# Pooled attention feeding a top-1 mixture of experts: one load moved forward, routing operations moved behind subtractions, one low-part subtraction moved to an earlier step, three more tiles stored undivided

## The chip, the cores and the metric

The kernel runs on one core of one Trainium2 chip. The metric is the device time of one execution in microseconds (us). Lower is better. The engines are named as in the profile: PE is TensorE (matrix products and transposes), DVE is VectorE, ACT is ScalarE, POOL is GpSimd, SP is SyncE, which here only issues DMAs. A DMA is a transfer between the chip's memory and an engine's memory.

## What is computed

The input q, k and v have 8 batches, 8 heads, 576 rows and 64 columns. Keys and values are averaged over groups of 8 rows, which leaves 72 of each. The attention's output is one row of 512 numbers for each of 4608 tokens. Each token then goes to the one expert of eight with the largest logit, through that expert's two matrices, and the result is scaled by the gate.

```python
k_p = k.reshape(B, H, Sp, 8, D).mean(axis=3)          # 72 pooled keys
v_p = v.reshape(B, H, Sp, 8, D).mean(axis=3)
scores = scale * np.matmul(q, k_p.transpose(0, 1, 3, 2))
scores = scores - np.max(scores, axis=-1, keepdims=True)
attn = np.exp(scores)
attn = attn / (np.sum(attn, axis=-1, keepdims=True) + 1e-09)
x = np.matmul(attn, v_p)                                # 4608 x 512 after a transpose
logits = x @ w_gate + modality_bias[modality_id]
e_idx = np.argmax(logits, axis=1)
probs = np.exp(logits - logits.max(-1, keepdims=True))
probs /= probs.sum(-1, keepdims=True) + 1e-09
gate_w = probs[np.arange(N), e_idx]
for e in range(8):
    mask = e_idx == e
    out[mask] = gate_w[mask, None] * (np.maximum(x[mask] @ w1[e], 0.0) @ w2[e])
```

## The kernel before, in words

The kernel has two stages that follow one another on PE. Roughly the first 180 us are attention and routing, the rest are the experts.

**Attention** runs in 20 steps, two batches to five steps. In each group of five, steps 0 and 1 are the two halves of the even batch, step 2 is a mixed step with the last 64 rows of both batches, and steps 3 and 4 are the halves of the odd batch. A step has two tiles of 128 tokens, a mixed step has one. Each step handles its scores in two halves of heads, w = 0 and w = 1. What a step does, with the names that the profile prints:

- `q_pe`, `q_act` transpose queries (`pq`, L578) and copy them (`qt`, L584).
- `s_pe` forms the scores (`sc`, L603; L597 in a mixed step).
- `s_dve` takes their maximum (`mx`, L610) and subtracts it (`sb`, L613) on DVE.
- `s_act` takes exponentials (`pe`, L625 and L626) on ACT.
- `t_pe`, `t_act` transpose them (`pp`, L632) and copy them (`pt`, L637). `t4_pe` transposes the remainder (L644) into free columns of the score tile of w = 0, so it waits until L613 has read that tile.
- `a_pe` multiplies with the values (`av`, L667 and L671). There is one `av` tile, so the next `a_pe` waits until `x_dve` has read the last one.
- `x_dve` reads `av`: the row sums (`r`, L690), their reciprocal (L694), the logits (`lg`, L696), and two multiplications that divide the rows (`xb`, L700). A tile called late skips L700: ACT copies the undivided rows (L692), the reciprocal is stored beside them in column RX and following, and the rows are multiplied by it after they have been gathered for an expert. L696 of a late tile comes after ACT's copy.

Keys and values of a batch are pooled mostly on POOL (`fold`, L351 to L353), partly on DVE (L356), and turned into operands on PE (`pk` L396 and L401, `pv` L443 and L444).

**The order of the work** is written out by hand. One loop over the steps calls these functions, and tables called hooks (`hook_0` to `hook_3`, `hook_q`) say what else is emitted at which point of which step. Every engine runs its instructions in the order in which they are emitted. The DMAs of all inputs are issued by SP, in one queue, from the table `step_loads`.

**Routing** of a group of nine tiles (one group for two batches) is some 30 small DVE operations. They stand in a list, `drip`. A call of `gap(n)` takes the next n of them and emits them at that place, unless the next one is held for PE. Group 0's list starts at step 6, group 1's at step 11, with a table for the first two slots of tokens behind it, group 2's at step 16. Group 3's is run in the expert stage.

**Experts.** Weights are used as two parts, a high part rounded on ACT (`split0`, L902) and a low part that DVE subtracts (`split_lo`, L141, 128x1024). The table over `hook_3` says in which step each of the eight pieces of the first expert has its low part made. From about 180 us on PE multiplies tokens in slots of 256, in the same pattern to the end (L183, L209, L214, L1345).

Of the kernel before, what the change touches and what calls it, by code (L numbers as in the profile page):

```python
# [14 lines left out]
AF = mybir.ActivationFunctionType  # L15
# [7 lines left out]
P = 128  # L23
SLOT = 256
EARLY_GROUPS = 2
# [8 lines left out]
def kernel(  # L34
# [12 lines left out]
    nc = tc.nc  # L47
# [3 lines left out]
    E, _, FF = w1.shape  # L51
# [187 lines left out]
    with ExitStack() as actx:  # L239
# [306 lines left out]
        def gap(n=2):  # L546

            for _ in range(n):
                if drip and drip[0] not in held:
                    drip.pop(0)()  # L550
# [55 lines left out]
        def s_dve(n, w):  # L606
            nh = 2 * len(steps[n][2])
            scv = scs.pop((n, w))[:, :, 0:nh * SPL].rearrange("p u (h s) -> p u h s", s=SPL)
            mx = ap.tile([P, 2, 4], F32, tag="mx", bufs=2, name=f"mx_{n}_{w}")[:, :, 0:nh]
            nc.vector.reduce_max(mx, scv, axis=AX.X)  # L610
            gap()
            sb = ap.tile([P, 2, 4 * SPL], F32, tag="sb", bufs=2, name=f"sb_{n}_{w}")
            nc.vector.tensor_tensor(sb[:, :, 0:nh * SPL].rearrange("p u (h s) -> p u h s", s=SPL), scv,  # L613
                                    mx.rearrange("p u (h o) -> p u h o", o=1).to_broadcast([P, 2, nh, SPL]), op=ALU.subtract)
            scs[n, w] = sb

        def s_act(n, w):
# [55 lines left out]
        def x_dve(t):  # L673
# [12 lines left out]

            late = g >= EARLY_GROUPS and z == 1
            r = xw[:, z, RX:RX + H].rearrange("p (u h) -> p u h", u=2) if late else s8
            rb = r.rearrange("p u (h o) -> p u h o", o=1)
            nc.vector.tensor_scalar(s8, avv[:, :, :, VC - 1], float(POOL), 1e-9 * POOL, op0=ALU.mult, op1=ALU.add)  # L690
            if late:
                nc.scalar.copy(xo.rearrange("p (u h d) -> p u h d", u=2, h=4), avv[:, :, :, 0:HD])  # L692
            gap(1)
            nc.vector.reciprocal(r, s8)  # L694
            gap(1)
            nc.vector.tensor_tensor(lgs[g][:, gi].rearrange("p (u h) e -> p u h e", u=2), avv[:, :, :, HD:HD + E],  # L696
# [34 lines left out]
        def route(g):  # L731
# [3 lines left out]
            lg = small("lgr", g, [P, n, E])  # L735
            ex = small("ex", g, [P, n, E])
            m1 = small("m1", g, [P, n])
# [8 lines left out]
            V = nc.vector  # L746
# [8 lines left out]
            def sub():  # L755
                V.tensor_tensor(lg, lg, per_e(m1, n), op=ALU.subtract)
                nc.scalar.activation(ex, lg, AF.Exp)
            add(sub)
# [20 lines left out]
            add(lambda: V.reduce_sum(sm, ex, axis=AX.X))  # L779
            add(lambda: V.tensor_scalar_add(sm, sm, 1e-9))  # L780
            add(lambda: V.reduce_sum(dc, oh[:, sl, :].rearrange("p t e -> p e t"), axis=AX.X))
# [134 lines left out]
        for f, n in enumerate((12, 13, 14, 15, 15, 16, 17, 19)):  # L916
            at(hook_1, n, lambda f=f: split0(f, 0))
            at(hook_2, n, lambda f=f: split0(f, 1))
        for f, n in enumerate((15, 15, 16, 16, 17, 17, 18, 19)):
            at(hook_3, n, lambda f=f: split_lo(f, nc.vector))  # L920
# [17 lines left out]
        step_loads = {}  # L938
        for n, fn, b in ((0, load_k, 2), (0, load_k4, 2), (0, load_v, 2), (0, load_v4, 2), (0, load_k, 3), (1, load_q, 2),
                         (1, load_v, 3), (1, load_k4, 3), (1, load_routing, None), (1, load_k, 4), (2, load_qmix, 1),  # L940
# [256 lines left out]
    for i, r in enumerate(EXTRA):  # L1197
# [14 lines left out]
    late = {  # L1212
        (0, 0): [lr[9], lr[7], lr[11], lr[8]],
        (0, 1): [lr[10]],
        (0, 3): [counts, lr[12]] + [fn for pair in zip(bases, lr[13:20]) for fn in pair] + lr[20:25],
        (0, 4): experts,
        (0, 5): lr[25:] + columns,
        (0, 6): first_cols[:3],
# [432 lines left out]
```

## Time and profile before

| | |
|---|---|
| three runs | 591.69, 593.76 and 594.55 us, median 593.76 |
| the profiled execution's own time | 590.98 us |
| its span, first to last instruction | 589.3 us |
| busy: PE, DVE, ACT, POOL | 97%, 63%, 46%, 32% |
| mean granted PE clock | 0.998 of full speed |

The profile lists instructions by engine, line and tile. A row of a timeline gives the start, the duration, the engine, the line, the operation, the tile written and the tiles read, the size and the count of merged instructions. In square brackets stands how long the engine sat idle before it, and whose work ended that. The view of waits sums these idle times. SP's rows are the issue of a DMA, not the transfer. In the order of the program, as against the trace, rows carry no time.

### The profile page before, as it was taken

How to read it: one execution, taken by the hardware profiler on the slowest of the kernel's cores; microseconds unless marked ns; L12 is line 12 of the kernel's file. 1: busy time of each engine (PE TensorE's matmuls, PEld its weight loads, DVE VectorE, ACT ScalarE, POOL GpSimd, SP SyncE). 2: the span in 40 equal slices, each digit the busy share in tenths (PEclk: the TensorE clock that was granted, in tenths of full speed). 3: DMA queues.
4: the chain of work that ended last, by engine and by line, in shares of the span. 5: the costliest groups of instructions: out<-in, count | busy, mean ns of one | idle time of the engine just before them, and what ended most of it. 6: DMA issues, size and time to landing. Idle time of an engine off the chain costs nothing.

```text
span 589.3 us, 12333 instructions
## 1 busy us (share of the span) xinstructions
PE 570.9 (97%) x3539; PEld 499.6 (85%) x3539; DVE 372.7 (63%) x945; ACT 273.8 (46%) x652; POOL 187.2 (32%) x290
## 2 busy tenths in 40 slices
PE   6999999999999999999999999999999999999995
PEld 5789789988898888888888888888888888888894
DVE  5877898788966766557455446855455487555311
ACT  2767677788552333333333336633333474334210
POOL 7679967765000323112112102112102113212101
PEclk9999999999999999999999999999999999999999
DMA  8999979995311744232232277242234843241101
GB/s 257 306 323 282 360 219 309 304 313 171 103 54 39 263 169 121 79 125 91 82 118 95 86 230 241 91 125 91 87 111 137 255 158 105 91 146 54 38 3 55
DMA packets 83426, 92.60 MB, mean 157 GB/s; under 512 B 17871, under 2 KB 58319, under 8 KB 83344
## 3 DMA queue, kind: packets, MB, share of 16 engines
q1 hardware_dynamic: 77424, 72.24, 39.2%
q0 software_dynamic: 5920, 19.44, 9.9%
q8 instruction: 30, 0.49, 0.4%
q14 instruction: 52, 0.43, 0.2%
HBM read 123.06 MB, written 27.58 MB: 256 GB/s over the span
## 4 chain that ended last, share of the span: by engine, by line
PE 82%; DVE 7%; DMA 5%; ACT 2%; issue 1%; SPq 1%; POOLq 0%; POOL 0%; DVEq 0%; ACTq 0%
PE op L1345 33%; PE hp L209 20%; PE hp L214 10%; PE av L667 4%; PE hp L183 3%; PE sc L603 3%; DMA q<-in_q_dram 3%; PE av L671 2%; DMA v<-in_v_dram 2%; PE pp L632 2%; PE pq L578 2%; PE ph L183 1%; DVE mx L610 1%; DVE hl L141 1%; DMA out_dram<-obw,slw 1%
## 5 line engine op out<-in xcount | busy, mean ns | idle before, releaser
L209 PE MATMUL hp<-xhl,hl 128*128 128x512 f32 x512 | 126.6, 390 | 0.0
L1321 POOL DMA_INDIRECT out_dram<-ob,sidx x34 | 36.8, 1083 | 263.6 <-DVE ob L1315 191.2
L209 PEld LDWEIGHTS hp<-xhl,hl 128*128 128x128 f32 x512 | 96.1, 188 | 19.9
L217 ACT COPY ht<-hp 128x256 f32<-128x256 f32 x128 | 47.3, 373 | 138.7 <-PE hp L214 112.3
L218 DVE TENSOR_TENSOR ht<-ht,hp 128x256 f32<-128x256 f32 x128 | 52.8, 420 | 92.5 <-ACT ht L217 89.4
L1345 PE MATMUL op<-hl,hx 128*128 128x512 f32 x429 | 104.8, 392 | 0.0
L1345 PEld LDWEIGHTS op<-hl,hx 128*128 128x128 f32 x429 | 78.5, 189 | 14.6
L1345 PE MATMUL op<-hl,hh 128*128 128x512 f32 x256 | 79.8, 393 | 0.0
L214 PEld LDWEIGHTS hp<-xhl,hl 128*128 128x128 f32 x512 | 69.8, 191 | 4.9
L214 PE MATMUL hp<-xhl,hl 128*128 128x256 f32 x512 | 71.5, 283 | 0.0
L1345 PEld LDWEIGHTS op<-hl,hh 128*128 128x128 f32 x256 | 46.0, 189 | 7.8
L667 PE MATMUL av<-vw,pt 128*128 128x146 f32 (+1 forms) x320 | 49.2, 293 | 1.4 <-DVE xb L700 1.3
L1345 PE MATMUL op<-hl,hlo 128*128 128x512 f32 x128 | 49.9, 390 | 0.0
L144 POOL DMA_INDIRECT xg<-xs,gidx x36 | 38.6, 1073 | 29.0 <-DMA raw<-in_moe_w_dram 13.8
L667 PEld LDWEIGHTS av<-vw,pt 128*128 128x128 f32 (+1 forms) x320 | 39.6, 180 | 3.4 <-DVE xb L700 1.0
L223 DVE SCALAR_TENSOR_TENSOR hx<-ht,hx 128x256 fp32r<-128x256 f32 x64 | 27.2, 427 | 18.8 <-DVEq L1350 15.7
L223 DVE SCALAR_TENSOR_TENSOR hlo<-ht,hh 128x256 fp32r<-128x256 f32 x64 | 27.1, 425 | 18.5 <-DVEq L1350 15.3
L603 PE MATMUL sc<-kt,qt 128*128 128x144 f32 x256 | 37.4, 289 | 0.6 <-DVE rs L798 0.3
L603 PEld LDWEIGHTS sc<-kt,qt 128*128 128x128 f32 x256 | 33.2, 190 | 1.6 <-DVE rs L798 0.5
L610 DVE TENSOR_REDUCE mx<-sc 128x8 f32<-128x576 f32 (+1 forms) x40 | 27.7, 692 | 7.5 <-PE sc L603 6.9
L671 PE MATMUL av<-vw,pt 128*128 128x146 f32 (+1 forms) x160 | 30.0, 290 | 0.0
L221 ACT ACTIVATE hx<-ht 128x256 fp32r<-128x256 f32 x64 | 26.2, 419 | 7.4 <-DVE ht L218 5.7
(279 smaller groups left out, 907.7 us busy)
## 6 DMA issues: line engine op xcount, KB each, us to landing
raw<-in_moe_w_dram SPq DMA_DIRECT2D x288, 256.0 KB
xs<-xb SPq DMA_DIRECT2D x16, 528.0 KB
scr<-xg SPq DMA_DIRECT2D x29, 256.0 KB
k<-in_k_dram SPq DMA_DIRECT2D x7, 1024.0 KB
v<-in_v_dram SPq DMA_DIRECT2D x7, 1024.0 KB
q<-in_q_dram SPq DMA_DIRECT2D x7, 1024.0 KB
y<-scr SPq DMA_DIRECT2D x108, 64.0 KB
v<-in_v_dram SPq DMA_DIRECT2D x16, 128.0 KB
```

Source lines behind the costliest of these rows:

```text
L144: nc.gpsimd.indirect_dma_start(out=x, out_offset=None, in_=xs[0:rows, :], in_offset=IndirectOffsetOnAxis(idx[:, col:col + 1].bitcast(U32), 0),
L209: nc.tensor.matmul(hp[g % 2], hl[g][:, 0, d * P:(d + 1) * P], ab[:, d, :, 0:SLOT], start=(d == 0), stop=False)
L214: nc.tensor.matmul(hp[g % 2][:, 0:SLOT], hl[g][:, 1, d * P:(d + 1) * P], ab[:, d, 0, 0:SLOT], start=False, stop=(d == ND - 1))
L217: nc.scalar.copy(hts[g % 2], hp[g % 2][:, SLOT:2 * SLOT])
L218: nc.vector.tensor_add(hts[g % 2], hts[g % 2], hp[g % 2][:, 0:SLOT])
L223: nc.vector.scalar_tensor_tensor(hlo, hts[g % 2], 0.0, hh.bitcast(F32), op0=ALU.max, op1=ALU.subtract)
L603: nc.tensor.matmul(dst, qt[:, i, :], kt[b % NB][:, :, h * SPL:(h + 1) * SPL], start=True, stop=True)
L610: nc.vector.reduce_max(mx, scv, axis=AX.X)
L667: nc.tensor.matmul(av[hs, u, 2 * VC * gg:2 * VC * (gg + 1)], pt[:, c, hs], vw[y][:, c].rearrange("p a x -> p (a x)"), start=(gg == 0), sto ...
L671: nc.tensor.matmul(dst4[hs], pt4[:, hs], v4[y][:, 2 * u:2 * u + 2, :], start=False, stop=True)
L1321: nc.gpsimd.indirect_dma_start(out=out[:, :], out_offset=IndirectOffsetOnAxis(idx.bitcast(U32), 0), in_=ob, in_offset=None, bounds_check=N ...
L1345: nc.tensor.matmul(ot, l[:, ts_], hl[f][:, w, D:2 * D], start=(f == 0 and n == 0), stop=(f == NF - 1 and n == 2))
```

## The change

Six edits, all in the attention stage and its routing:

1. **Loads.** The queries of batch 2 (`load_q`, 2) are issued ahead of the keys of batch 3 (`load_k`, 3). Before, the keys stood in step 0's row and the queries in step 1's.
2. **`s_dve`.** For w = 0 the two routing operations of `gap()` come behind the subtraction L613; before they stood between the maximum and the subtraction. For w = 1 nothing changes.
3. **`x_dve`.** Two routing operations come ahead of the row sums, in place of one behind the row sums and one behind the reciprocal. The two at the function's end stay.
4. **Late tiles.** The first tile of the last three steps (17, 18 and 19) is late too: its two multiplications L700 go, a copy on ACT comes.
5. **Routing.** The small constant added to the sum of exponentials (L780) goes. The tile `ex` gets a ninth column with that constant, which POOL writes when the group's list is made, and the sum (L779) runs over nine columns.
6. **Low parts.** The first of the eight low-part subtractions moves from step 15 to step 13. The others shift with it: steps 13, 15, 15, 16, 16, 17, 18, 19 in place of 15, 15, 16, 16, 17, 17, 18, 19, so step 17 has one in place of two.

```diff
@@ s_dve
             nc.vector.reduce_max(mx, scv, axis=AX.X)
-            gap()
+            if w:
+                gap()
...
             scs[n, w] = sb
+            if w == 0:
+                gap()
@@ x_dve
-            late = g >= EARLY_GROUPS and z == 1
+            late = g >= EARLY_GROUPS and (z == 1 or n >= N - 3)
...
+            gap(2)
             nc.vector.tensor_scalar(s8, avv[:, :, :, VC - 1], float(POOL), 1e-9 * POOL, op0=ALU.mult, op1=ALU.add)
...
-            gap(1)
             nc.vector.reciprocal(r, s8)
-            gap(1)
@@ route
-            ex = small("ex", g, [P, n, E])
+            ex = small("ex", g, [P, n, E + 1])
+            nc.gpsimd.memset(ex[:, :, E:E + 1], 1e-9)
...
-                nc.scalar.activation(ex, lg, AF.Exp)
+                nc.scalar.activation(ex[:, :, 0:E], lg, AF.Exp)
...
-            add(lambda: V.tensor_scalar_add(sm, sm, 1e-9))
@@ the tables
-        for f, n in enumerate((15, 15, 16, 16, 17, 17, 18, 19)):
+        for f, n in enumerate((13, 15, 15, 16, 16, 17, 18, 19)):
             at(hook_3, n, lambda f=f: split_lo(f, nc.vector))
...
-        for n, fn, b in (... (0, load_v4, 2), (0, load_k, 3), (1, load_q, 2),
+        for n, fn, b in (... (0, load_v4, 2), (1, load_q, 2), (1, load_k, 3),
```

The list of group 3, which runs in the expert stage, is one operation shorter as well, and its indices there shift by one.

What this does to the order of three queues follows. The lines of the changed kernel stand two or three numbers lower in the file: L614 there is L613 here, L694 is L690, L697 is L694, L702 is L700, L782 is L779, L783 is L781, L786 is L784, L794 is L792, L811 is L809.

DVE at the turn from step 6 to step 7, in group 0's routing, before: `mx` and `sb` are the maximum and subtraction of step 7, w = 0; `sm`, `dc`, `gate` and `cum` are routing; `r`, `lg` and `xb` belong to the second tile of step 5.

```order
L610 TENSOR_REDUCE mx_0_1100<-sc_0_1088 128x2x2
L779 TENSOR_REDUCE sm_1008<-ex_1005 128x9
L780 TENSOR_SCALAR sm_1008<-sm_1008 128x9
L613 TENSOR_TENSOR sb_0_1104<-sc_0_1088,mx_0_1100 128x2x144
L690 TENSOR_SCALAR r_1121<-av_1114 128x8
L781 TENSOR_REDUCE dc_1009<-oh 128x8
L694 RECIPROCAL r_1121<-r_1121 128x8
L784 RECIPROCAL gate<-sm_1008 128x9
L696 TENSOR_TENSOR lg_1071<-av_1114,r_1121 128x64
L700 TENSOR_TENSOR xb_171<-av_1114,r_1121 128x256 x2
L792 TENSOR_TENSOR cum<-cum,dc_1009 128x8
```

The same place in the changed kernel:

```order
L610 TENSOR_REDUCE mx_0_1101<-sc_0_1089 128x2x2
L614 TENSOR_TENSOR sb_0_1103<-sc_0_1089,mx_0_1101 128x2x144
L782 TENSOR_REDUCE sm_1009<-ex_1005 128x9
L783 TENSOR_REDUCE dc_1010<-oh 128x8
L786 RECIPROCAL gate<-sm_1009 128x9
L794 TENSOR_TENSOR cum<-cum,dc_1010 128x8
L694 TENSOR_SCALAR r_1122<-av_1115 128x8
L697 RECIPROCAL r_1122<-r_1122 128x8
L698 TENSOR_TENSOR lg_1072<-av_1115,r_1122 128x64
L702 TENSOR_TENSOR xb_171<-av_1115,r_1122 128x256 x2
```

The subtraction has moved two places forward. Four routing operations, `cum` among them, now stand between it and the row sums `r`, where one stood.

DVE at the turn from step 13 to step 14, before: `mx_0` and `sb_0` are step 14, w = 0, `mx_1` and `sb_1` are w = 1, `arow` is group 1's routing; where a line of dots stands, more rows of `arow` and the two short operations between `r` and `xb` are left out.

```order
L610 TENSOR_REDUCE mx_0_1931<-sc_0_1919 128x8
L809 TENSOR_SCALAR arow<-iota_b,rkf_1606 128x128 x2
L613 TENSOR_TENSOR sb_0_1935<-sc_0_1919,mx_0_1931 128x576
...
L610 TENSOR_REDUCE mx_1_1999<-sc_1_1968 128x8
...
L613 TENSOR_TENSOR sb_1_2003<-sc_1_1968,mx_1_1999 128x576
L690 TENSOR_SCALAR r_2018<-av_1992 128x8
...
L700 TENSOR_TENSOR xb_175<-av_1992,r_2018 128x256 x2
```

The same place in the changed kernel; `hl` is the low part of the first piece of weights:

```order
L610 TENSOR_REDUCE mx_0_1931<-sc_0_1919 128x8
L614 TENSOR_TENSOR sb_0_1933<-sc_0_1919,mx_0_1931 128x576
L811 TENSOR_SCALAR arow<-iota_b,rkf_1607 128x128 x4
L141 TENSOR_TENSOR hl_1764<-raw_1508,hl_1764 128x1024
L610 TENSOR_REDUCE mx_1_2000<-sc_1_1969 128x8
...
L614 TENSOR_TENSOR sb_1_2004<-sc_1_1969,mx_1_2000 128x576
```

The subtraction of w = 0 moves ahead of two `arow` operations, and a subtraction of 128x1024 stands between the two halves.

SP around the change of the loads, in the changed kernel; `q_414` are the queries of batch 2, `k_416` the keys of batch 3:

```order
L272 DMA v_348<-in_v_dram 128x4x512
L278 DMA v_2_350<-in_v_dram 64x1x512 x2
L290 DMA q_414<-in_q_dram 128x8x256
L257 DMA k_416<-in_k_dram 128x4x512
L272 DMA v_418<-in_v_dram 128x4x512
L264 DMA k_3_420<-in_k_dram 64x512
```

Before, the two middle rows stood the other way round. Nothing else in SP's queue up to here has moved. Later one store of attention rows falls behind group 2's four stores of gates. On PE no instruction has moved. POOL has four more small writes, and ACT has three more copies.

More of the change, by code (lines that the diff above doesn't have):

```diff
@@ L938 @@
         step_loads = {}
-        for n, fn, b in ((0, load_k, 2), (0, load_k4, 2), (0, load_v, 2), (0, load_v4, 2), (0, load_k, 3), (1, load_q, 2),
+        for n, fn, b in ((0, load_k, 2), (0, load_k4, 2), (0, load_v, 2), (0, load_v4, 2), (1, load_q, 2), (1, load_k, 3),
                          (1, load_v, 3), (1, load_k4, 3), (1, load_routing, None), (1, load_k, 4), (2, load_qmix, 1),
@@ L1212 @@
     late = {
-        (0, 0): [lr[9], lr[7], lr[11], lr[8]],
-        (0, 1): [lr[10]],
-        (0, 3): [counts, lr[12]] + [fn for pair in zip(bases, lr[13:20]) for fn in pair] + lr[20:25],
+        (0, 0): [lr[8], lr[7], lr[10]],
+        (0, 1): [lr[9]],
+        (0, 3): [counts, lr[11]] + [fn for pair in zip(bases, lr[12:19]) for fn in pair] + lr[19:24],
         (0, 4): experts,
-        (0, 5): lr[25:] + columns,
+        (0, 5): lr[24:] + columns,
         (0, 6): first_cols[:3],
```

## Prediction

> **What bounds the kernel now.** I read the page first, then what PE waited for, then stretches of 10 us, then PE's timeline at every wait, and last the engines that ended those waits.
>
> The page, its head and the busy times:
>
> ```profile
> span 589.3 us, 12333 instructions
> ...
> PE 570.9 (97%) x3539; PEld 499.6 (85%) x3539; DVE 372.7 (63%) x945; ACT 273.8 (46%) x652; POOL 187.2 (32%) x290
> ```
>
> PE is idle for 589.3 - 570.9 = 18.4 us in all. Three stretches show where: each row gives the length, then the busy time of PE, its weight loads, DVE, ACT and POOL, then the granted clock, the DMA engines' share and GB/s.
>
> ```profile
> 30.00:40.00 10.00, 9.82 (x90) 9.16 (x90) 8.14 (x18) 7.01 (x19) 7.11 (x12) 1.00 1.06 316
> ...
> 150.00:160.00 10.00, 8.99 (x89) 7.88 (x88) 9.34 (x27) 5.48 (x13) 0.00 (x0) 1.00 0.23 70
> ...
> 300.00:310.00 10.00, 10.00 (x53) 8.60 (x52) 4.96 (x14) 3.16 (x8) 0.00 (x0) 1.00 0.33 107
> ```
>
> In the expert stage PE has no idle time, at full clock, and the change touches no product there. Whatever the change brings or costs is the sum of PE's waits in the attention stage. The largest, from the view of PE's waits (total, times, longest):
>
> ```profile
> PE pk L396 <- POOL kt L327: 4.8, 1, 4.8
> PE pq L578 <- DMA q<-in_q_dram: 1.7, 2, 1.1
> PE sc L644 <- DVE sb L613: 1.5, 3, 0.5
> ```
>
> The first is the start and stays. The change can touch eight places of PE's timeline; in brackets is the wait:
>
> ```profile
> 43.48 0.63 PE L578 MATMUL pq<-ident,q 128*128 128x128 f32 x4 [1.09 <-DMA q<-in_q_dram]
> ...
> 69.44 0.33 PE L644 MATMUL sc<-ident,pe 128*128 128x128 f32 x1 [0.54 <-DVE sb L613]
> ...
> 70.83 0.74 PE L667 MATMUL av<-vw,pt 128*128 128x146 f32 x4 [0.62 <-DVE xb L700]
> ...
> 84.37 0.30 PE L644 MATMUL sc<-ident,pe 128*128 128x128 f32 x1 [0.49 <-DVE sb L613]
> ...
> 122.08 0.30 PE L644 MATMUL sc<-ident,pe 128*128 128x128 f32 x1 [0.49 <-DVE sb L613]
> ...
> 151.89 0.77 PE L667 MATMUL av<-vw,pt 128*128 128x146 f32 x4 [0.72 <-DVE xb L700]
> ...
> 158.63 1.25 PE L603 MATMUL sc<-kt,qt 128*128 128x144 f32 x8 [0.28 <-DVE rs L798]
> ...
> 163.28 0.66 PE L632 MATMUL pp<-ident,pe 128*128 128x128 f32 x4 [0.54 <-DVE h L187]
> ```
>
> Their sum, 1.09 + 0.54 + 0.62 + 0.49 + 0.49 + 0.72 + 0.28 + 0.54 = 4.77 us, is the most that can be won. It is 0.8% of 593.76 us. About 0.5%, 2.97 us, is what a measurement of this kernel can tell from no change.
>
> **The change part by part.** Gains are written with a plus.
>
> *The queries of batch 2.* The chain of waits gives their landing, SP's timeline the issues, and those of DVE, PE and POOL what is late next:
>
> ```profile
> 27.43 15.92 DMA q<-in_q_dram
> ```
> ```profile
> 26.75 0.58 SPq L257 DMA_DIRECT2D k<-in_k_dram  x1
> 27.43 1.27 SPq L290 DMA_DIRECT2D q<-in_q_dram  x1
> ```
> ```profile
> 43.97 1.07 DVE L356 TENSOR_REDUCE vp<-v 128x64 f32<-128x512 f32 x1
> ```
> ```profile
> 45.48 0.38 PE L443 MATMUL pv<-ident,vp 128*128 128x128 f32 x2
> ...
> 53.76 0.49 PE L396 MATMUL pk<-ident,kp 128*64 128x128 f32 x3
> ```
> ```profile
> 43.17 1.28 POOL L351 TENSOR_TENSOR k<-k 128x512 f32<-128x512 f32 x1
> ```
>
> The queries landed at 27.43 + 15.92 = 43.35, about 15 us behind their issue. So the queue is backed up and a place in it decides. The keys just ahead, 128x4x512 numbers of 4 bytes, are as large as the queries, 1.05 MB. At the 316 GB/s of the first stretch above that is 3.3 us, so the queries should land near 40. PE wants them at 43.48 - 1.09 = 42.39, and this wait goes. Next late is `pv`: its second transpose needs the DVE reduction that ends at 43.97 + 1.07 = 45.04. The row at 45.48 holds both transposes, the second about 0.1 later; without the wait PE would come to it at 45.6 - 1.1 = 44.5. So 0.5 of the 1.09 us are won, **+0.5** (bounds 0 and 1.09). The keys land where the queries did, 43.35. POOL's fold began at 43.17, so it starts 0.2 us late; PE's transposes of these keys are at 53.76, some 10 us on, and hide it. Without that cover it would cost the 0.2.
>
> *Routing behind the subtraction and ahead of the row sums.* This is one edit with two signs. The subtraction comes earlier, which releases L644. But four routing operations now run between it and `r`, `lg` and `xb`, and the tile `av` comes free at the end of those. Before, three of the four stood in the short gaps between dependent operations, where they cost little. At group 0, steps 6 and 7, DVE's and POOL's rows:
>
> ```profile
> 68.14 0.89 DVE L780 TENSOR_SCALAR sm<-sm 128x9 f32<-128x9 f32 x1
> ...
> 69.38 0.27 DVE L781 TENSOR_REDUCE dc<-oh 128x8 f32<-128x72 bf16 x1
> ...
> 70.60 0.65 DVE L792 TENSOR_TENSOR cum<-cum,dc 128x8 bf16<-128x8 bf16 x1
> ...
> 150.13 0.10 DVE L792 TENSOR_TENSOR cum<-cum,dc 128x8 bf16<-128x8 bf16 x1
> ```
> ```profile
> 69.16 1.27 POOL L351 TENSOR_TENSOR v<-v 128x512 f32<-128x512 f32 x1
> 70.51 0.73 POOL L352 TENSOR_TENSOR v<-v 128x256 f32<-128x256 f32 x1
> ```
>
> L780 goes, 0.89 us. Ahead of `r` come L781, the gate's reciprocal (about as long as L781 at most) and L792. L792 works on 8 numbers and yet took 0.65 us, from 70.60 to 71.25. POOL's L352 ended at 70.51 + 0.73 = 71.24. So L792 ended with POOL's operation, as if it had waited for it, and a wait for L351 in its place would be 1.27. Its cost lies between the 0.10 that it took at 150.13, with POOL idle, and 1.27; I take the measured 0.65. The Trainium skill, "SBUF — State Buffer", section "SBUF: two separate sides", says that DVE and POOL share a port pair under an exclusive lock, held for a whole instruction, which a DVE operation with two SBUF inputs needs against a POOL operation that reads SBUF, and that the loser blocks fully. By that rule, the trace agrees: 71.25 against 71.24; and the sum would be lower by up to 0.6 in each group whose L792 comes just behind the start of an L351.
>
> Before, L792 stood behind `xb`, and its wait held up nobody on PE. Now it stands in `av`'s chain. The balance at group 0: L780 -0.89; L781 0.27, the reciprocal 0.2, and L792 0.65 as measured, together 1.12; and the pair ahead of the first tile's `r` at step 6, taken out of its gaps, 0.2. That is 0.4 us later. The sum L779 now waits for POOL's write into `ex`, which stands in POOL's queue ahead of the operation before the L351 above, so at about 68.5; DVE gets to L779 at about that time, behind the subtraction. If POOL is late, DVE waits, for up to one operation of 0.73. The wait of 0.54 at L644 goes, but it is followed by the wait at 70.83 which takes all of it back and the lateness too: **-0.4** (bounds -1.2 and +0.5).
>
> Step 9 loses its wait at L644 (84.37), and only two `arow` operations come ahead of its `r`. I take the slack behind it to be that of step 14, 1.13 us below, where the same operations stand: **+0.5** (bounds 0 and 0.5).
>
> Group 1, steps 11 and 12: no wait on PE before. The same four operations stand ahead of a late tile's `r`, and behind `r` in ACT's queue stand the copy L692 and then the copy `pt` that PE needs. The price is L792's again, 0.1 to 1.27, and part of it is covered by the subtraction's coming earlier; I take half of 0.65: **-0.3** (bounds -1.0 and 0).
>
> The table of the first slots, step 15, and its neighbours on PE:
>
> ```profile
> 132.88 0.29 DVE L866 TENSOR_TENSOR sc<-oh,e0oh 128x144 f32<-128x144 bf16 x1
> ...
> 133.21 0.30 DVE L867 TENSOR_REDUCE s<-sc 128x18 f32<-128x144 f32 x1
> ...
> 133.56 0.75 DVE L700 TENSOR_TENSOR xb<-av,r 128x256 f32<-128x256 f32 x2
> ```
> ```profile
> 134.59 0.67 PE L667 MATMUL av<-vw,pt 128*128 128x146 f32 x4
> ```
>
> `av` was free at 133.56 + 0.75 = 134.31, and PE came 0.28 us later. Now L866 and L867 run ahead of `r`, 0.29 + 0.30, of which the gaps held some 0.1: 0.5 later, 0.2 more than the slack: **-0.2** (bounds -0.5 and 0).
>
> Group 2, step 17. ACT's exponential of the logits waits for a routing subtraction that now comes behind L613:
>
> ```profile
> 144.81 0.26 ACT L757 ACTIVATE ex<-lgr 128x72 f32<-128x72 f32 x1 [1.43 <-DVE lgr L756]
> ```
>
> ```profile
> 144.70 0.45 DVE L613 TENSOR_TENSOR sb<-sc,mx 128x288 f32<-128x288 f32 x1
> ```
>
> That is 0.45 us, and ACT had nothing else to do: everything behind the exponential on ACT, this step's `pt` too, moves by it. The wait of 0.72 at 151.89 follows and absorbs most: **-0.15** (bounds -0.6 and +0.3).
>
> *The first low part at step 13.* Its duration, in a stretch in which POOL does nothing (above), and the two rows that it now comes ahead of:
>
> ```profile
> 163.47 1.22 DVE L141 TENSOR_TENSOR hl<-raw,hl 128x1024 fp32r<-128x1024 f32 x1
> ```
> ```profile
> 125.57 0.74 DVE L700 TENSOR_TENSOR xb<-av,r 128x256 f32<-128x256 f32 x2
> ```
> ```profile
> 127.44 0.77 PE L667 MATMUL av<-vw,pt 128*128 128x146 f32 x4
> ```
>
> `av` was free at 126.31, PE came at 127.44: a slack of 1.13. The wait at 122.08 goes (+0.49), so PE comes at 126.95. DVE, which has no idle time there, is later by 1.22 and by 0.2 for two `arow` ahead of `r`: 127.73. PE waits 0.75, more than it won: **-0.25** (bounds -1.0, if L141 waits for POOL as well, and +0.5).
>
> *The end of the stage.* Step 17 has one L141 less, and the first tiles of steps 17 to 19 lose two L700. DVE is 1.22 earlier at 158.63 and more at 163.28, so both waits go, 0.28 + 0.54 = +0.82. If another operation took their cover, the 0.82 would stay. But the ACT copy queues behind `pt` in steps 19 and 20:
>
> ```profile
> 168.42 0.59 ACT L637 COPY pt<-pp 128x512 f32<-128x512 f32 x1 [1.55 <-PE pp L632]
> ```
> ```profile
> 169.66 0.66 PE L667 MATMUL av<-vw,pt 128*128 128x146 f32 x4
> ```
>
> It starts at about 169.0, takes 0.59 as the same shape does here, and the logits behind it 0.2, so `av` is free at 169.8 and PE loses 0.15, twice: **+0.5** (bounds 0 and 0.8).
>
> *At nothing:* POOL's four small writes otherwise, and the store that SP now issues behind group 2's gates, since PE waits for no store in this stage.
>
> Sum: 0.5 - 0.4 + 0.5 - 0.3 - 0.2 - 0.15 - 0.25 + 0.5 = +0.2 us. The profiled execution took 590.98 us, 1.7 beyond its span and 2.8 under the median of the three runs, and would take 590.8. On the median this is **593.6 us**.
>
> **The rivals.** *All eight waits go and nothing is late behind them.* Then DVE's gaps before `r` are filled for free, as far as DVE waits there for PE: 593.76 - 4.77 = 589.0. For it speaks that DVE is busy for 63% only. Against it speak three places where DVE has no idle time, above.
>
> *The lock's losses stand in `av`'s chain.* Each operation with two SBUF inputs that has come ahead of `r`, L792 twice and L141 once, waits for a whole POOL operation. By the lower bounds, with the loads' and step 9's gains kept: 0.5 - 1.2 + 0.5 - 1.0 - 0.5 - 0.6 - 1.0 + 0 = -3.3, so 597.1. It decides from L792 at 0.65 upward in both groups. For it speaks that POOL runs folds without pause there; against it, that each loss also lets PE come later to the next place.
>
> *The load's swap does nothing,* if the queries wait for a free tile and not for the queue, or the later keys make POOL late. Then +0.5 goes: 594.0. The backlog of 15 us speaks against it.
>
> **How the numbers follow.** The forecast, a sum within 2 us of zero, has 0.72; the gain of all waits 0.14; the lock's losses 0.10; the idle swap 0.04. Runs of the same kernel spread from 591.69 to 594.55, 1.4 to each side. Range: 590.8, halfway into the first rival's case, to 596.3, most of the way to the second's. Faster by over 0.5%, under 590.8: 0.13, nearly all of the first rival. Slower, over 596.7: 0.06, the greater half of the second. Within: 0.81.
>
> **What would show it.** Right: no wait of PE for `q` after 43 us, but one for `pv` behind L356; no wait at L644; waits at L667 at about 70, 127 and 134 us; none for L798 and L187; L792 with a POOL operation's end at its own. Wrong: the expert stage starting over 2 us earlier or later than before (its first L1345 at 180.86), or new waits of PE in it.

## The result and the profile after

| | before | changed |
|---|---|---|
| median of 22 runs each | 591.61 us | 595.43 us |
| ratio to before, 95% interval | 1 | 1.0064 (1.0045 to 1.0083) |
| profiled execution, own time | 590.98 us | 598.26 us |
| its span | 589.3 us | 596.5 us |
| its mean granted PE clock | 0.998 | 0.995 |

The change makes the kernel 0.64% slower, 3.8 us; the forecast was no change. That 595.43 us lies between the forecast's 590.8 and 596.3 is luck: those bounds were laid on a median of three runs, 593.76, and over 22 runs the kernel before has 591.61. Measured from the kernel before, the upper bound was 2.5 us away. The profiled execution of the changed kernel is the longest of its 22 runs: its trace shows where time goes, and the ratio how much of it stays on average. Its head and PE's busy time:

```profile
span 596.5 us, 12336 instructions
...
PE 573.2 (96%) x3539; PEld 499.2 (84%) x3539; DVE 374.1 (63%) x935; ACT 275.2 (46%) x655; POOL 187.9 (31%) x294
```

PE's idle time is now 596.5 - 573.2 = 23.3 us, against 18.4, and PE is busy 2.3 us longer for the same 3539 instructions. The view of PE's waits (total, times, longest) shows the first. PE's lines have moved too: `av` L670, the transposes L647 and L635 are L667, L644 and L632 of before. In the other kernels below they differ by a few again, and the tiles say which row is which.

```profile
PE av L670 <- DVE xb L702: 6.2, 5, 3.3
...
PE sc L647 <- DVE sb L614: 0.9, 1, 0.9
...
PE sc L597 <- ACT vg L467: 0.7, 1, 0.7
...
PE pv L443 <- POOL k L351: 0.5, 1, 0.5
```

Waits for `av` have gone from 1.3 to 6.2 us. The three waits for `sb` of before are gone (the 0.9 is another, at 31 us). PE's timeline at the waits for `av` and at two others:

```profile
74.52 1.08 PE L670 MATMUL av<-vw,pt 128*128 128x146 f32 x4 [3.34 <-DVE xb L702]
...
99.34 0.74 PE L670 MATMUL av<-vw,pt 128*128 128x146 f32 x4 [1.06 <-DVE xb L702]
...
134.03 0.77 PE L670 MATMUL av<-vw,pt 128*128 128x146 f32 x4 [0.45 <-DVE xb L702]
...
142.11 0.77 PE L670 MATMUL av<-vw,pt 128*128 128x146 f32 x4 [0.77 <-DVE xb L702]
...
153.75 0.71 PE L597 MATMUL sc<-kt,qt 128*64 128x144 f32 x8 [0.68 <-ACT vg L467]
...
159.92 0.77 PE L670 MATMUL av<-vw,pt 128*128 128x146 f32 x4 [0.56 <-DVE xb L702]
...
170.36 0.66 PE L635 MATMUL pp<-ident,pe 128*128 128x128 f32 x4 [0.25 <-DVE h L187]
```

The longest stands at group 0, at the turn from step 6 to 7. DVE's rows there, and POOL's:

```profile
69.57 0.46 DVE L614 TENSOR_TENSOR sb<-sc,mx 128x288 f32<-128x288 f32 x1
71.16 0.24 DVE L782 TENSOR_REDUCE sm<-ex 128x9 f32<-128x81 f32 x1 [1.14 <-POOL ex L739]
...
71.62 1.51 DVE L794 TENSOR_TENSOR cum<-cum,dc 128x8 bf16<-128x8 bf16 x1
73.06 0.15 DVE L694 TENSOR_SCALAR r<-av 128x8 f32<-128x8 f32 x1
...
73.63 0.74 DVE L702 TENSOR_TENSOR xb<-av,r 128x256 f32<-128x256 f32 x2
```
```profile
71.02 0.11 POOL L739 MEMSET ex<- 128x9 f32 x1
...
71.86 1.26 POOL L351 TENSOR_TENSOR v<-v 128x512 f32<-128x512 f32 x1
```

The sum of exponentials, L782, waits 1.14 us for POOL's write of the ninth column, which stands in POOL's queue behind the folds of the keys. Then `cum`, 8 numbers, takes 1.51 us and ends at 73.13, with POOL's L351 (73.12). Both stand ahead of `r`, so `av` comes free late and PE idles 3.34 us. What follows is seen in stretches of 5 us (length, busy time of PE, its weight loads, DVE, ACT, POOL, granted clock, DMA share, GB/s):

```profile
70.00:75.00 5.00, 1.66 (x16) 1.25 (x13) 3.69 (x12) 1.92 (x6) 4.69 (x10) 0.98 1.04 368
75.00:80.00 5.00, 5.00 (x31) 4.98 (x31) 2.18 (x7) 1.19 (x4) 4.61 (x8) 0.68 1.08 346
```

PE is busy throughout the second stretch. Its 31 instructions take 5.56 us from the first's start to the last's end; the same 31 took 3.89 us before. The four products at 74.52 take 1.08 us, against 0.74 at 99.34. The clock is at half for 3.41 us, from 74.77 to 78.18, another 1.7 us lost. The Trainium skill, "TensorE: Matmul & The Clock Gate", section "What's actually happening", says that the array runs at half its clock after an idle window of about 3.4 us and until it has been busy for such a window. The trace agrees with the halving and with its length; on how much idle time it takes, see below.

The next place is step 10, of which the prediction did not speak: DVE ahead of the wait at 99.34, then the same place in the kernel before, where L824 to L827 are L822 to L825, then POOL in the changed kernel.

```profile
95.66 0.76 DVE L614 TENSOR_TENSOR sb<-sc,mx 128x576 f32<-128x576 f32 x1
96.33 0.55 DVE L824 TENSOR_SCALAR rot<-iota_f,e 128x8 f32<-128x8 f32 x1
96.92 0.17 DVE L825 TENSOR_SCALAR t<-rot 128x8 f32<-128x8 f32 x1
97.12 0.58 DVE L826 TENSOR_TENSOR rot<-rot,t 128x8 f32<-128x8 f32 x1
97.73 0.23 DVE L827 TENSOR_TENSOR lmat<-rot 128x64 f32<-128x64 f32 x1
97.88 0.16 DVE L694 TENSOR_SCALAR r<-av 128x8 f32<-128x8 f32 x1
```
```profile
90.13 0.75 DVE L613 TENSOR_TENSOR sb<-sc,mx 128x576 f32<-128x576 f32 x1
91.52 0.17 DVE L690 TENSOR_SCALAR r<-av 128x8 f32<-128x8 f32 x1 [0.64 <-PE av L671]
91.60 0.33 DVE L824 TENSOR_TENSOR rot<-rot,t 128x8 f32<-128x8 f32 x1
...
92.24 0.75 DVE L700 TENSOR_TENSOR xb<-av,r 128x256 f32<-128x256 f32 x2
```
```profile
95.59 1.27 POOL L351 TENSOR_TENSOR v<-v 128x512 f32<-128x512 f32 x1
96.94 0.74 POOL L352 TENSOR_TENSOR v<-v 128x256 f32<-128x256 f32 x1
```

Before, DVE stood idle 0.64 us here and `r` began when PE had `av` ready. Now four operations on 8 to 64 numbers run between the subtraction and `r`, 1.46 us from 96.42 to 97.88. Two of them end with a POOL operation: L824 at 96.88 (L351 at 96.86), L826 at 97.70 (L352 at 97.68). `av` was free 0.18 us ahead of PE before (92.99 against 93.17), so nearly all of it is a wait. No run took POOL's folds away from a place like this; that DVE waits for POOL rests on ends that agree, here and at groups 0 and 1, to 0.03 us.

The table shows the places against the prediction. It compares the start of the same PE instruction in two traces, in a quiet stretch behind a place, less the same ahead of it, in us, plus for later. (The quiet points lie at 40, 49, 80, 86, 96, 110, 129.5, 136.5, 155 and 180.5 us of before.) The columns behind the changed kernel belong to two experiments: edits 2 and 3 alone, and edits 1, 4, 5 and 6 with the early write of the column. A dash is a place with less than 0.05.

| place (us in before) | predicted | changed | edits 2, 3 | the other four |
|---|---|---|---|---|
| queries of batch 2 (43 to 48) | -0.5 | -0.62 | -0.48 | -0.64 |
| group 0, steps 6 and 7 (69 to 78) | +0.4 | +3.72 | -0.19 | -0.79 |
| step 9 (84) | -0.5 | -0.41 | -0.41 | - |
| step 10 (93) | not named | +1.26 | +1.27 | - |
| group 1 (108) | +0.3 | +0.19 | +0.98 | - |
| step 13, low part (122, 127) | +0.25 | +0.20 | -0.32 | - |
| table (134) | +0.2 | +1.03 | +0.31 | - |
| group 2 (145, 151) | +0.15 | +0.41 | +0.68 | -0.15 |
| end of the stage (158 to 178) | -0.5 | -0.43 | +0.46 | -0.93 |
| sum | -0.2 | +5.35 | +2.29 | -2.49 |

The changed kernel's trace is 7.68 us later at PE's last instruction. Of that, 2.26 arise in the first 31 us (1.13 by 13 us, where PE waits for queries, and the `sb` wait of 0.9). They are that run's: the trace of edits 2 and 3 alone, whose loads stand as before, loses 0.65 at 13 us too, and the wait at 31 us is in no other trace. Nor does the first row belong to edit 1. All five traces of kernels with the loads as before (edits 2 and 3, edit 2, edit 3, edits 4 and 6, edit 5) win 0.47 to 0.63 there without the swap, and their waits for `q` are 0.62, 0.14, 0.26, 0.63 and none. In the last, edit 5 alone, PE's row has no wait:

```profile
42.98 0.63 PE L578 MATMUL pq<-ident,q 128*128 128x128 f32 x4
```

So the wait of 1.09 us in the profile before is not in every run.

### The profile page after: what moved, and what is told of

Its sections match the earlier page's. It is cut to its first block, busy times and chain, and to the rows that moved or that the text cites. A ratio compares the mean times of both kernels' runs of the same rounds, so it can differ in the third digit from the quotient of the medians.

```text
span 596.5 us, 12336 instructions
## 1 busy us (share of the span) xinstructions
PE 573.2 (96%) x3539; PEld 499.2 (84%) x3539; DVE 374.1 (63%) x935; ACT 275.2 (46%) x655; POOL 187.9 (31%) x294
## 4 chain that ended last, share of the span: by engine, by line
PE 77%; DVE 10%; DMA 6%; POOL 3%; issue 2%; ACT 1%; SPq 0%; POOLq 0%; DVEq 0%; ACTq 0%
PE op L1347 33%; PE hp L209 20%; PE hp L214 10%; DMA k<-in_k_dram 5%; PE av L670 3%; PE hp L183 3%; PE sc L603 2%; PE av L674 2%; DVE sb L614 1%; DVE mx L610 1%; PE ph L183 1%; DVE xb L702 1%; DVE hl L141 1%; PE pp L635 1%; DMA out_dram<-obw,slw 1%
## 5 line engine op out<-in xcount | busy, mean ns | idle before, releaser
L209 PE MATMUL hp<-xhl,hl 128*128 128x512 f32 x512 | 128.2, 392 | 0.0
L670 PE MATMUL av<-vw,pt 128*128 128x146 f32 (+1 forms) x320 | 50.3, 297 | 6.7 <-DVE xb L702 6.2
L670 PEld LDWEIGHTS av<-vw,pt 128*128 128x128 f32 (+1 forms) x320 | 40.2, 182 | 9.5 <-issue 3.7
L674 PE MATMUL av<-vw,pt 128*128 128x146 f32 (+1 forms) x160 | 30.6, 294 | 0.0
L614 DVE TENSOR_TENSOR sb<-sc,mx 128x576 f32<-128x576 f32 (+1 forms) x40 | 27.8, 696 | 2.3
```

Source lines behind the costliest of these rows:

```text
L209: nc.tensor.matmul(hp[g % 2], hl[g][:, 0, d * P:(d + 1) * P], ab[:, d, :, 0:SLOT], start=(d == 0), stop=False)
L670: nc.tensor.matmul(av[hs, u, 2 * VC * gg:2 * VC * (gg + 1)], pt[:, c, hs], vw[y][:, c].rearrange("p a x -> p (a x)"), start=(gg == 0), sto ...
L674: nc.tensor.matmul(dst4[hs], pt4[:, hs], v4[y][:, 2 * u:2 * u + 2, :], start=False, stop=True)
```

## The experiments

Theory 1, from the profile: POOL's write and `cum` at group 0, with the halved clock behind them, are the loss. Rival A: it is the low part and the table. Rival B: it is the later start. After the first four runs a theory 2 took the place of theory 1: what costs is that routing stands ahead of the row sums, wherever it does (edits 2 and 3), and the write and the clock make it worse at group 0. All runs were compared with the kernel before on the same chip. Ratios are to it, with the 95% interval.

**Parts of the changed kernel undone.** First, POOL's column written early:

```diff
-            nc.gpsimd.memset(ex[:, :, E:E + 1], 1e-9)   # in route(g)
+            for g in range(len(GROUPS)):                # in routing_constants()
+                exs.append(... .tile([P, GT, E + 1], F32, name=f"ex_{g}"))
+                nc.gpsimd.memset(exs[g][:, :, E:E + 1], 1e-9)
```

> The changed kernel, but the ninth columns of the four `ex` tiles are written by POOL at the program's start, in tiles of their own; routing adds no write to POOL's queue any more. Theory 1 (group 0: DVE's sum L782 waits 1.14 us for POOL's write, then cum L794 waits 1.51 us ahead of the row sums, PE waits 3.3 us for av and its clock is halved for 3.7 us): the wait at L782 goes, PE's wait for av at about 71 us falls to 2.2 or less, or cum falls against another POOL operation; no halved clock behind it; in all 2.5 to 4 us faster than the changed kernel, ratio to the kernel before 0.998 to 1.003. Rival A (the low part at step 13 and the table of the first slots carry the loss): the time stays, ratio 1.005 to 1.008. Rival B (the start, 2.3 us later by 31 us, carries it): the time stays, 1.005 to 1.008.

Measured 1.0025 (1.0005 to 1.0044), 592.88 us. PE and DVE at group 0:

```profile
70.86 0.74 PE L673 MATMUL av<-vw,pt 128*128 128x146 f32 x4 [0.79 <-DVE xb L705]
```
```profile
69.29 0.19 DVE L796 TENSOR_TENSOR cum<-cum,dc 128x8 bf16<-128x8 bf16 x1
```

DVE gets through before POOL's next fold starts, `cum` takes 0.19, PE's wait falls from 3.34 to 0.79, and no halved clock follows. As theory 1 expected; rivals A and B fall. But 0.25% stays.

Second, edit 5 undone, so that POOL writes nothing and DVE adds the constant:

```diff
-            ex = small("ex", g, [P, n, E + 1])
-            nc.gpsimd.memset(ex[:, :, E:E + 1], 1e-9)
+            ex = small("ex", g, [P, n, E])
...
+            add(lambda: V.tensor_scalar_add(sm, sm, 1e-9))
```

> The changed kernel with edit 5 undone: eight columns, the constant added on DVE again, no write of POOL. Theory 1: the wait for POOL's write is gone, but the addition on DVE (0.89 us before, beside POOL) stands again, now ahead of the row sums; so PE's wait for av at 71 us is 2 to 3.3 us, near the bound at which the clock fell, and the gain is smaller or less certain than with the early write: ratio to the kernel before 0.999 to 1.006. Rivals A and B: ratio 1.005 to 1.008.

Measured 1.0050 (1.0032 to 1.0068), 593.7 us. That lies in theory 1's range and at the edge of the rivals', so the time does not part them, and the wait of 2 to 3.3 us did not come: the list is one operation longer, so `cum` falls behind `xb` at group 0 and PE's wait there is 0.97. At group 1 PE loses 1.0 instead. Most of the loss remains without any write of POOL: theory 1 was too narrow.

Third, edit 3 undone:

```diff
-            gap(2)
             nc.vector.tensor_scalar(s8, avv[:, :, :, VC - 1], ...)
...
+            gap(1)
             nc.vector.reciprocal(r, s8)
+            gap(1)
```

> The changed kernel with edit 3 undone: one routing operation behind the row sums and one behind the reciprocal, none ahead. Theory 1: cum L794 falls behind xb or between the dependent operations again, the 1.51 us that it waits for POOL no longer stands wholly ahead of r; PE's wait for av at 71 us falls under 2.5 us, no halved clock; the waits at 98 and 134 us get shorter too; ratio to the kernel before 0.996 to 1.002. Rival A: the table's wait at 134 us shrinks by at most 0.5, the low part's stays, ratio 1.004 to 1.007. Rival B: 1.005 to 1.008.

Measured 1.0013 (0.9996 to 1.0031), 591.76 us: most of the loss goes. The wait at 71 us is 1.83, since `cum`, between the reciprocal and the logits, still waits 1.3 us for POOL; the one at 134 us is gone, the one at 93 us is 0.63 instead of 1.06.

Fourth, edit 6 undone:

```diff
-        for f, n in enumerate((13, 15, 15, 16, 16, 17, 18, 19)):
+        for f, n in enumerate((15, 15, 16, 16, 17, 17, 18, 19)):
```

> The changed kernel with edit 6 undone: the low parts at steps 15, 15, 16, 16, 17, 17, 18, 19. Theory 1: only PE's wait of 0.66 to 0.75 at 127 us goes, and up to 0.8 comes back at 158 and 163 us; the wait of 3.3 us at 71 us and the clock behind it stay; ratio to the kernel before 1.004 to 1.008. Rival A: the loss goes, 0.998 to 1.003. Rival B: 1.005 to 1.008.

Measured 1.0067 (1.0040 to 1.0093), 595.64 us, in 7 runs: the loss is not the low part's. Its trace shows the clock again; first PE's wait, then the stretches behind it:

```profile
71.93 1.31 PE L670 MATMUL av<-vw,pt 128*128 128x146 f32 x4 [2.25 <-DVE xb L702]
```
```profile
70.00:72.00 2.00, 0.07 (x1) 0.10 (x1) 1.93 (x7) 0.49 (x1) 1.84 (x4) 0.98 1.06 377
72.00:75.00 3.00, 3.00 (x13) 2.99 (x14) 0.61 (x2) 0.00 (x0) 2.84 (x4) 0.50 1.05 385
```

An idle time of 2.25 us was followed by the half clock, where the 1.83 in the trace with edit 3 undone was not.

**Edits alone, on the kernel before.** Edit 1:

```diff
-  (0, load_v4, 2), (0, load_k, 3), (1, load_q, 2),
+  (0, load_v4, 2), (1, load_q, 2), (1, load_k, 3),
```

> The kernel before with edit 1 alone: the queries of batch 2 ahead of the keys of batch 3. Theory (PE's wait at 43 us is won, the transpose of the values behind it takes half of it back): 0.5 to 0.7 us faster, ratio to the kernel before 0.998 to 1.000, with PE's wait for q at 43 us gone and one of 0.5 for pv behind it. Rival B (the swap makes the first steps later by what the four traces of changed kernels showed at 13 us, 0.3 to 1.1 us): the gain is eaten, 1.000 to 1.001.

Measured 0.9990 (0.9971 to 1.0010), as the theory expected, though the interval does not exclude rival B. PE's wait at 43 us is gone, and one of 0.45 for `pv` stands behind it. But the same comes without the swap (see the table's first row), and this trace loses 1.80 us in its first 20 us, in waits for earlier queries; edit 3 alone, whose loads stand as before, loses 1.59 there. So what the swap is worth is open, and small.

Edits 2 and 3:

```diff
-            gap()
+            if w:
+                gap()
...
+            if w == 0:
+                gap()
...
+            gap(2)
             nc.vector.tensor_scalar(s8, avv[:, :, :, VC - 1], ...)
...
-            gap(1)
             nc.vector.reciprocal(r, s8)
-            gap(1)
```

> The kernel before with edits 2 and 3 alone: the routing operations behind the subtraction and ahead of the row sums, no write of POOL, the constant still added on DVE. Theory 2 (what costs is that routing stands ahead of the row sums, at group 0, at the rotations of step 10, at the table and at group 2): waits of about 1 us at 93 us, 0.4 at 134, 0.7 at 145, against 0.4 won at 84 and 0.45 at 122: 1 to 2.5 us slower, ratio 1.0015 to 1.004. Theory 1 in its narrow form (only POOL's write into ex makes the order costly): the three waits for sb go and little comes, 0.997 to 1.000.

Measured 1.0048 (1.0032 to 1.0065): more than theory 2 expected, since group 1 costs 0.98. There DVE's addition comes just behind the start of a fold of POOL:

```profile
106.78 0.90 DVE L782 TENSOR_SCALAR sm<-sm 128x9 f32<-128x9 f32 x1
```
```profile
106.38 1.27 POOL L351 TENSOR_TENSOR v<-v 128x512 f32<-128x512 f32 x1
```

It ends at 107.68, the fold at 107.65; before, the same addition took 0.17 there. The delay of `r` reaches PE by way of ACT's copies. These two edits alone bring 0.48 of the 0.64%, and their trace has no halved clock.

Edit 2 alone (the first half of the diff above), then edit 3 alone (the second half):

> The kernel before with edit 2 alone: for w = 0 the two routing operations behind the subtraction; the gaps behind the row sums and the reciprocal as before. Theory 2, by the run with edit 3 undone: 0.5 won at 69 and up to 0.5 lost at 71, 0.4 won at 84, 0.5 to 0.8 lost at 93, 0.5 won at 122, 0.5 lost at 145: within 0.7 us of before, ratio 0.999 to 1.0015. If edit 2 alone carries the loss: 1.003 to 1.005.

> The kernel before with edit 3 alone: two routing operations ahead of the row sums, the two of w = 0 ahead of the subtraction as before. Theory 2 (the loss needs both: only what the subtraction passes and what stands ahead of the row sums together is more than the slack): 0.3 to 1 us lost, at 108 and 134 above all, little at 93 and 145: ratio 1.0005 to 1.002. If edit 3 alone carries the loss: a wait of 1.2 at 93 us as well, 1.003 to 1.005.

Measured 1.0004 (0.9981 to 1.0027) and 1.0022 (0.9999 to 1.0044). At the places of the table, edit 2 wins 0.35 at group 0, 0.41 at step 9 and 0.32 each at group 1 and step 13, and loses 0.83 at step 10 and 1.02 at group 2. Edit 3 loses 0.19 at group 0, 0.36 at step 10, 0.17 at group 1, 0.33 at the table and 0.32 at the end; its trace also has a half clock early, from 15.27 to 18.68 us, behind a wait of 1.40 for queries. That the loss needs both, as theory 2 had it, holds at group 1 (0.98 together, -0.32 and +0.17 apart); at step 10 the two single losses nearly add up to the 1.27. The two intervals also hold a plain sum of the two edits.

Edits 4 and 6 alone:

```diff
-            late = g >= EARLY_GROUPS and z == 1
+            late = g >= EARLY_GROUPS and (z == 1 or n >= N - 3)
...
-        for f, n in enumerate((15, 15, 16, 16, 17, 17, 18, 19)):
+        for f, n in enumerate((13, 15, 15, 16, 16, 17, 18, 19)):
```

> The kernel before with edits 4 and 6 alone: three more late tiles, the first low part at step 13. By the places seen so far: the waits at 158 and 163 us go, 0.8 to 1.0; two copies on ACT cost 0.24 each at 170 and 178; the low part costs 0.1 to 0.2 at 127, where the subtraction's gain of 0.45 is missing: 0.2 to 0.4 us faster, ratio to the kernel before 0.998 to 1.000. Rival A (the low part waits for POOL, or the copies delay more): 1.001 to 1.003.

Measured 0.9999 (0.9974 to 1.0023). The trace wins 1.29 at 158 and 163 us, more than was expected, and loses 0.69 at 170 and 178; the interval is too wide to see it.

Edit 5 alone:

```diff
+            ex = small("ex", g, [P, n, E + 1])
+            nc.gpsimd.memset(ex[:, :, E:E + 1], 1e-9)
...
-            add(lambda: V.tensor_scalar_add(sm, sm, 1e-9))
```

> The kernel before with edit 5 alone: the ninth column and POOL's write, no addition on DVE; the order of routing as before. Theory 2 (the write costs only where it stands ahead of the row sums): the sum waits 0.5 to 1.1 us for POOL's write ahead of the subtraction, the addition of 0.89 is gone, so PE at 70 us comes within 0.5 of before, ratio 0.999 to 1.001. Theory 1 (the write itself costs): 1.002 to 1.005, with a wait of PE over 2 us and a halved clock at 71 us.

Measured 1.0007 (0.9988 to 1.0025): the write costs little where routing stands in its old places. At 71 us PE comes 0.77 later than before, more than the 0.5 that was expected, with a wait of 1.31 and no halved clock in the trace.

**Is it the idle time that halves the clock?** The changed kernel, PE kept at work in the wait at 71 us:

```diff
-            for c in range(NPAIR):
+            for c in list(range(NPAIR)) * times:
                 nc.tensor.transpose(pp[:, c, :], ...)
...
-                t_pe(old[1])
+                t_pe(old[1], 5 if n == 7 else 1)
```

> The changed kernel with PE kept at work in its wait at 71 us: the four transposes ahead of it (step 7, the second tile of step 6) run five times, with the same data into the same place, 2 us more work that ends before av comes free. If the idle stretch of 2.2 to 3.3 us halves PE's clock behind it: no granted clock under 1 between 70 and 80 us, hardly a run with a mean clock of 0.995 or less, and 1 to 1.8 us faster than the changed kernel although PE does more: ratio to the kernel before 1.003 to 1.005. If the clock falls there for another reason: halved as before, ratio 1.0055 to 1.009.

Measured 1.0034 (1.0017 to 1.0051), 593.31 us. PE does 16 transposes more, and by the two ratios the kernel is 0.3% faster than the changed kernel (0.05 to 0.55% by their intervals). PE's rows, then the stretch:

```profile
68.30 2.35 PE L635 MATMUL pp<-ident,pe 128*128 128x128 f32 x20
71.08 0.74 PE L670 MATMUL av<-vw,pt 128*128 128x146 f32 x4 [0.44 <-DVE xb L702]
```
```profile
75.00:80.00 5.00, 5.00 (x62) 4.58 (x61) 4.03 (x13) 2.88 (x7) 2.17 (x3) 1.00 0.98 313
```

The mean clock of a run was 0.995 or less in 14 of 22 runs of the changed kernel, in none of 11 here, in 2 of 12 with the early write, in none of 12 with edit 5 undone, in 4 of 12 with edit 3 undone, in 4 of 7 with edit 6 undone and in 6 of 111 of the kernel before. It was so in 4 of 12 with edit 3 alone, 3 of 12 with edit 5 alone and 7 of 12 of the run that follows, all three with waits of 1.3 to 1.6 us in their traces, and in one run at most of each of the others. The 14 took 596.0 us on average, the other eight 594.0. So the halved clock follows from the idle time. Its share of the loss of 3.8 us, as an estimate, is 1.3 us by the 14 runs (2.0 us in 14 of 22) and 1.8 by the filled wait, a third to a half.

**What can be won.** Edit 1, and edit 2 in the two steps where its gain had slack behind it:

```diff
+            if w or n not in (9, 14):
+                gap()
...
+            if w == 0 and n in (9, 14):
+                gap()
```

> The kernel before with edit 1, and with edit 2 only in steps 9 and 14, where the subtraction's gain had slack behind it; nothing ahead of the row sums. Theory 2: the waits at 43, 84 and 122 us go, 0.6 + 0.4 + 0.45 = 1.5 us faster, ratio 0.9965 to 0.9985. If each gain is given back by the next wait: 0.999 to 1.001.

Measured 0.9994 (0.9978 to 1.0010): no gain. The profiled execution is the longest of the 12; its waits show what came in its place, 6.1 us for queries in five places, and the clock falls about 1 us behind one of them (PE's row, then two stretches of 1 us):

```profile
PE pq L578 <- DMA q<-in_q_dram: 6.1, 5, 1.6
```
```profile
105.44 0.63 PE L578 MATMUL pq<-ident,q 128*128 128x128 f32 x4 [1.60 <-DMA q<-in_q_dram]
```
```profile
106.00:107.00 1.00, 1.00 (x8) 0.89 (x7) 1.00 (x6) 0.65 (x2) 0.00 (x0) 0.75 1.06 403
107.00:108.00 1.00, 1.00 (x5) 1.00 (x6) 0.32 (x1) 0.47 (x3) 0.45 (x2) 0.50 1.06 415
```

Then the four edits that do not move routing, with the column written early, and the same with edit 2 in steps 9 and 14 (diffs as above):

> The kernel before with edits 1, 4, 5 and 6, the ninth columns written at the program's start; edits 2 and 3 left out, so routing stands where it stood. Theory 2 (the order of routing carries the whole loss, and what the other edits win is small): by the places 0.7 won at 43 us, 0 to 0.5 at 69, 0.4 at the end of the stage, ratio to the kernel before 0.997 to 0.9995; no halved clock at 71 us. If the queries' transfers take back what is won ahead of 105 us: 0.999 to 1.001. If another edit carries part of the loss: 1.002 or more.

> The run above with edit 2 in steps 9 and 14 as well. Theory 2: the waits for sb at 84 and 122 us go; behind the second stands the low part of step 13, so 0.4 to 0.6 us more than the run above, ratio 0.996 to 0.9985. If the queries' transfers take it back: as the run above, 0.999 to 1.001, with a wait of PE for q of about 1 us or more at 82 or 104 us.

Measured 0.9942 (0.9921 to 0.9964), 588.26 us, and 0.9943 (0.9923 to 0.9962), 588.42 us, in 6 and 7 runs. Both are faster than the kernel before and the changed kernel, and by more than was expected. At group 0 of the first the wait for `sb` is gone, and so is the addition of 0.89 on DVE; `av`, with a wait of 0.44 against 0.62 before, gives none of it back (-0.79 there, where the late write of edit 5 alone cost 0.77):

```profile
68.96 0.74 PE L670 MATMUL av<-vw,pt 128*128 128x146 f32 x4 [0.44 <-DVE xb L703]
```

Its trace is 2.87 us earlier at PE's last instruction, 2.49 of it at the places in the table. The kernel with the early write (1.0025) differs from this one by edits 2 and 3 alone. So beside the other four edits these two cost about 0.8%, more than the whole loss, and none of the other four carries it by itself; the late write of edit 5 makes it larger where routing has moved. The effects do not add up: edits 1, 4 and 6, and 5 alone measured 0.9990, 0.9999 and 1.0007. At group 0 the early write accounts for 1.56 us (0.77 + 0.79) of the 0.58%, which is 3.4 us; where the rest comes from is open. Whether the selected places of edit 2 are worth anything is not settled: the second trace waits for `q` 1.2 us in all, so the queries take back less than in the run before, but its time is the first's.

## Why the prediction was wrong

- *Queries of batch 2, +0.5*: the wait went, and one of 0.5 for `pv` took back what was said, but that it fits is luck. The wait of 1.09 belonged to one run's transfers and was taken for the kernel's: without the swap PE wins as much there. Alone, the edit measured 0.9990, an interval that holds no change.
- *Group 0, -0.4*: here it failed first. The step was "DVE gets to L779 at about that time ... for up to one operation of 0.73", and "I take the measured 0.65" for `cum`. POOL's queue was further behind: the wait was 1.14 and `cum` 1.51, longer than L351 alone (1.26). Both fell together, and the bound of -1.2 did not add them up. The 0.89 of L780, counted as won, was no price of L780 either. It ended at 69.03, and POOL's row of before ended at 69.00:

```profile
68.39 0.61 POOL L438 TENSOR_TENSOR vw<-vp,m 128x256 f32<-128x256 f32 x1
```

  At group 1 the same addition took 0.17. Taking it out left POOL's queue to be waited for by the next operation.
- *What the wait itself does to PE* had no term. The half clock behind it cost 1.7 us in the trace, and on average 1.3 to 1.8 us of the loss of 3.8.
- *Step 9, +0.5*: right, 0.41.
- *Step 10*: left out. "But four routing operations now run between it and `r`" was priced in the steps of `cum` and at the table, not where the rotations run. 1.26 to 1.28 us in every kernel with both edits; the row of DVE's idle 0.64 and the slack of 0.18 stood in the trace of before.
- *Group 1, -0.3*: 0.19 in the changed kernel, but 1.0 where the addition stands ahead as well. The size hangs on when POOL's fold starts.
- *The table, -0.2*: 1.03. The durations were taken from before, 0.29 for L866. Now L867 and L868, which are L865 and L866 of before, take 0.66 and 0.78 in place of 0.35 and 0.29. L867 ends at 139.12, POOL's L352 at 139.10; L868 ends 0.17 behind a fold's end, so that it waited is likely and not shown:

```profile
138.46 0.66 DVE L867 SCALAR_TENSOR_TENSOR adjv<-adjv,e0oh 128x8 f32<-128x8 f32 x1
...
139.71 0.78 DVE L868 TENSOR_TENSOR sc<-oh,e0oh 128x144 f32<-128x144 bf16 x1
```

- *Group 2, -0.15*: 0.41. "The wait of 0.72 at 151.89 follows and absorbs most" failed: it absorbed 0.16 and still measures 0.56.
- *The low part, -0.25, and the end of the stage, +0.5*: right, -0.20 and +0.43, the late copies costing about 0.3 each where 0.15 was said.
- *The rivals*: "the lock's losses stand in `av`'s chain" had the right mechanism and sign. Its 597.1, on a median of 593.76, is 3.3 us over before, and 3.8 was measured, but that is in part luck: it laid 1.0 each on group 1 and the low part, which cost 0.2, and had no half clock and no step 10. It had a chance of 0.10 because `cum` and the low part alone were counted as open to POOL's operations, and because "each loss also lets PE come later to the next place". That failed: the losses at 71, 93, 127, 134 and 145 us stand beside each other in the table, and only 0.16 was absorbed.

## What to carry to other kernels

A small operation moved ahead of a release is not priced by its length: beside a busy engine that it can wait for, it costs what is left of that engine's operation, so count every operation that has come ahead, at every step where the moved code runs. A wait of PE has a second price behind it, so a bound on waits that come together should add the half clock, 1.7 us here. A wait for a transfer can belong to one run: look for it in a second trace before counting it as a gain. A write that is needed late can be put early, out of a full queue: here that took back 0.4% of the 0.6%, and leaving routing where it stood as well gave a kernel 0.6% faster than before.

## What was not expected of the hardware

PE's clock fell to half in four traces: behind idle times of 3.34, 2.25 and 1.60 us, and of 1.40 us with edit 3 alone. Each time it stayed at 0.50 for 3.41 us. It did not fall behind 1.83 us with edit 3 undone, nor behind 1.71 us with edit 1 alone, so the length of one idle time does not decide; what does is open. The Trainium skill, "TensorE: Matmul & The Clock Gate", section "🎯 Why this matters for your kernels", advises against idle gaps over about 3 us; here half of that was enough in some runs. A DVE operation that reads one tile was held until POOL's operation ended as well: the addition L782 on 128x9 numbers took 0.90 us with edits 2 and 3 alone and ended within 0.03 us of a fold's end. It goes the other way too: in the changed kernel POOL's L352 on 64x128 numbers, which started 0.10 us behind DVE's low part of 1.21 us, took 1.42 us, against 0.45 in the profile before.
